# Blocks of one chunk from each sequence in a fused state-space and feed-forward kernel, with its first decays spread by TensorE

## The chip, the cores and the metric

The kernel runs on one core of a Trainium2 chip. The metric is the device time of one execution in microseconds; the span of a profile (first to last instruction) is about 1.8 us shorter than the time of the same execution.

## The reference

Two stages. The first is a scan over sequences (4 sequences, 8 heads, 768 positions, head dimension 32, state 16); the second a mixture of four feed-forward networks on its 3072 rows of 256.

```python
# stage 1, for each chunk; the result does not depend on the chunk length
L = np.exp(cum[:, :, :, None] - cum[:, :, None, :]) * causal   # products of decays a
M = np.einsum('bhin,bhjn->bhij', Cc, Bc) * L
y = np.einsum('bhij,bhjd->bhid', M, xc)                        # from within the chunk
y += np.einsum('bhin,bhnd->bhid', Cc, state) * decay_to_i      # from the chunks before it
state = decay_full * state + np.sum(Bx, axis=2)
# stage 2
p = domain_probs / (domain_probs.sum(-1, keepdims=True) + 1e-09)
for e in range(4):
    out += p[:, e:e + 1] * (np.maximum(x @ w1[e], 0.0) @ w2[e])
```

All is float32. Only the last line of stage 1 ties a chunk to the one before it, and only within a sequence.

## The kernel before

The kernel cuts the sequences into 24 chunks of 128 positions (6 for each sequence) and works in 6 blocks of 4 chunks, 512 rows. While block k goes through stage 2, the chunks of block k+1 go through stage 1 between its products. Stage 2 takes 8 weight steps a block. From the third step on it forms a 2 by 2 block product with seven products instead of eight, for which sums of weights are needed. GpSimd (POOL in the profile) makes these once, in block 0, and stores them for the later blocks. The first two steps of block 0 use eight plain products, because the sums are not there yet.

```python
    def sums_of(op):                       # POOL, 16 times (8 steps, two weight matrices)
        nc.gpsimd.tensor_add(op(S1), op(S3), op(A22))
        nc.gpsimd.tensor_sub(op(S2), op(S1), op(A11))
        nc.gpsimd.tensor_sub(op(S4), op(A12), op(S2))
        nc.gpsimd.tensor_sub(op(S3), op(A11), op(S3))

    def load_decays(c, queue):             # 8 heads x 128 decays, broadcast to 128 partitions: 512 KB
        ab = load.tile([P, NH * P], FP32, tag="ab", name="ab")
        nc.sync.dma_start(out=ab, in_=cut[c].rearrange("h s -> (h s)").partition_broadcast(P))
        if c % chunks_per_seq:             # decays by rows, only where a state comes in
            ...
    def decays(c):
        ...
        nc.vector.tensor_tensor_scan(out=LT, data0=s["ab"], data1=ident..., op0=mult, op1=add)
        ...                                # DVE: products of decays, 2.29 us
        if c % chunks_per_seq:
            nc.vector.tensor_tensor_scan(out=dec, data0=s["ah"], data1=zeros, initial=1.0, ...)
            nc.gpsimd.tensor_mul(cts, s["ctm"], dec...)

    def outputs(c, pool, tag):
        first = c % chunks_per_seq == 0
        if not first:                      # the "state product", 2 records on TensorE
            nc.tensor.matmul(out=y[:, :, 0:P], lhsT=state["M"]..., rhs=s["cts"], ...)
        for t in range(NT):
            for q in range(NQ):            # 16 records
                nc.tensor.matmul(out=y[32 * q:32 * q + 32, t, 0:w], lhsT=xb[...], rhs=MT[...], ...)
        nc.scalar.copy(out=yT[k][...], in_=y[:, :, 0:P])
```

A record is one entry of the profile; each float32 product of TensorE leaves two here.

The opening of the program, where TensorE has nothing to do but wait for the first chunks:

```python
    store_decays(); masks(0)
    turn(2)                # "turn" is a warm-up product whose result nobody reads
    scores(0, homes)
    turn(1)
    ...
    decays(0); masked(0, range(NQ)); masks(1); outputs(0, ...); store_gates()
    scores(1, homes)
    turn(3)
    decays(1); carry(0); masked(1, range(NQ)); masks(2); outputs(1, ...)   # carry: the state
    scores(2, homes)
    plain_first(0, 1)      # the first feed-forward product
```

And the end, where both halves of the last copy read one PSUM tile:

```python
        nc.vector.tensor_copy(rows[0][:, 0], turned[0][:, 0])
        nc.sync.dma_start(out=dst(0)[:, 0], in_=rows[0][:, 0])
        nc.scalar.copy(out=rows[0][:, 1], in_=turned[0][:, 1])
        nc.scalar.dma_start(out=dst(0)[:, 1], in_=rows[0][:, 1])
```

## Time and profile before

| | before |
|---|---|
| time, median of 3 runs | 662.41 us (661.87 to 662.48) |
| span of the profile | 659.3 us |
| TensorE busy | 647.0 us of it (98%) |
| first feed-forward product starts | 19.56 us |
| first half of the plain products over | 37.45 us |
| last products done, first transposition of the result starts | 653.09 us |
| last copy and store issue | 655.84 and 656.24 us |

Four marks of this table return for every run: the **first product**, the **half** (the start of the fourth group of plain first products, where the first 24 second products are over), the sum of the **waits** of TensorE for DVE between 45 and 118 us (block 0; here 0.15 + 0.87 + 0.30 + 0.64 + 0.16 = 2.12 us), and the **end mark**, the first transposition of the result. Since TensorE is busy nearly throughout, a microsecond that moves one mark should move all later ones. The lines of the page and of the opening are in the prediction; its 2.0 for output stores and 4.4 for a 96 KB load are us from issue to landing.

### The profile page before, as it was taken

The page shows a single profiled execution, that of the slowest core. Times are in us where ns is not written, and L with a number is a line of the kernel's source. Part 1 is how long each engine was busy: PE and PEld are TensorE (multiplying, and loading weights), DVE is VectorE, ACT ScalarE, POOL GpSimd, SP SyncE. Part 2 cuts the span into 40 slices and gives each one's busy share as a digit, 9 for nine tenths or more (in the row PEclk, how much of TensorE's full clock was granted, in tenths as well). Part 3 has the DMA queues.
Part 4 walks back from the last instruction along what each step waited for, and adds up shares of the span by engine and source line. Part 5 has one row for each costly group of instructions (what it writes and reads, how often), then busy time and mean ns, then how long its engine had stood idle before and what let it go on. Part 6 is the DMA issues. An engine that isn't in the chain of part 4 may idle for free.

```text
span 659.3 us, 8708 instructions
## 1 busy us (share of the span) xinstructions
PE 647.0 (98%) x3341; PEld 538.3 (82%) x3341; DVE 490.4 (74%) x787; ACT 115.3 (17%) x246; POOL 111.6 (17%) x153
## 2 busy tenths in 40 slices
PE   7999999999999999999999999999999999999997
PEld 2787887888888888888888888888888888888886
DVE  6857898788677688776778867768967776856655
ACT  2101111122112121121122111112211212111110
POOL 2487795030000002000003000001100000200000
PEclk9999999999999999999999999999999999999999
DMA  8975998646736444855372855554573443463100
GB/s 274 344 309 216 301 377 319 218 161 188 264 121 256 160 163 102 309 213 180 127 262 81 263 191 196 204 182 146 163 280 148 153 175 152 114 247 151 56 1 32
DMA packets 67145, 128.62 MB, mean 195 GB/s; under 512 B 24736, under 2 KB 48672, under 8 KB 67104
## 3 DMA queue, kind: packets, MB, share of 16 engines
q1 hardware_dynamic: 64208, 112.92, 50.3%
q0 software_dynamic: 2304, 14.68, 5.5%
q8 instruction: 26, 0.43, 0.2%
q10 hardware_dynamic: 592, 0.48, 0.2%
q14 instruction: 15, 0.12, 0.1%
HBM read 109.99 MB, written 18.07 MB: 194 GB/s over the span
## 4 chain that ended last, share of the span: by engine, by line
PE 87%; DVE 7%; issue 1%; DMA 1%; ACT 0%; DVEq 0%; SPq 0%
PE acc L440 39%; PE X L356 22%; PE Y L356 18%; DVE hT L385 2%; PE acc L421 2%; PE g L273 2%; PE y L301 1%; DVE MT L283 1%; DVE LT L239 1%; PE y L295 1%; DMA wt<-w_d 1%; PE X L404 1%; PE Y L404 1%; DVE z L368 1%; DVE h L378 1%
## 5 line engine op out<-in xcount | busy, mean ns | idle before, releaser
L440 PE MATMUL acc<-hT,wt 128*128 128x256 f32 x736 | 183.2, 382 | 0.0
L368 DVE TENSOR_TENSOR z<-Y,snap 128x512 f32<-128x512 f32 x138 | 95.0, 688 | 112.5 <-ACT snap L363 87.7
L363 ACT COPY snap<-X 128x512 f32<-128x512 f32 x138 | 80.9, 586 | 469.3 <-PE X L356 467.3
L440 PEld LDWEIGHTS acc<-hT,wt 128*128 128x128 f32 x736 | 138.2, 190 | 24.3 <-issue 6.3
L356 PE MATMUL X<-yS,wt 128*128 128x256 f32 x552 | 141.7, 379 | 0.0
L440 PE MATMUL acc<-h,wt 128*128 128x256 f32 x552 | 141.5, 379 | 0.0
L356 PEld LDWEIGHTS X<-yS,wt 128*128 128x128 f32 x552 | 104.9, 190 | 14.3
L440 PEld LDWEIGHTS acc<-h,wt 128*128 128x128 f32 x552 | 104.9, 190 | 14.3
L378 DVE SCALAR_TENSOR_TENSOR h<-z,gate 128x512 f32<-128x512 f32 x138 | 98.1, 711 | 3.2
L356 PE MATMUL Y<-yT,wt 128*128 128x256 f32 x368 | 94.8, 380 | 0.7 <-DVE z L368 0.6
L356 PEld LDWEIGHTS Y<-yT,wt 128*128 128x128 f32 x368 | 68.6, 190 | 12.3 <-DVE z L368 1.5
L385 DVE TENSOR_TENSOR hT<-h,hT 128x512 f32<-128x512 f32 x92 | 70.7, 768 | 3.2
L385 DVE TENSOR_TENSOR hT<-h,h 128x512 f32<-128x512 f32 x92 | 62.7, 717 | 0.7
L246 POOL TENSOR_TENSOR MT<-xb,LT 128x128 f32<-128x128 f32 x20 | 8.3, 415 | 317.1 <-issue 142.4
L239 DVE TENSOR_TENSOR_SCAN LT<-ab,ident 128x1024 f32<-128x1024 f32 x24 | 55.9, 2329 | 0.4
L356 PE MATMUL Y<-yS,wt 128*128 128x256 f32 x184 | 49.4, 391 | 2.0 <-DVE z L368 1.9
L283 DVE TENSOR_TENSOR MT<-g,LT 128x256 f32<-128x256 f32 x96 | 33.9, 415 | 20.9 <-PE g L273 20.8
L356 PE MATMUL X<-yT,wt 128*128 128x256 f32 x184 | 47.3, 380 | 0.9 <-DVE MT L283 0.9
L378 DVE SCALAR_TENSOR_TENSOR h<-X,gate 128x512 f32<-128x512 f32 x50 | 34.5, 691 | 10.4 <-PE X L356 5.7
L356 PEld LDWEIGHTS Y<-yS,wt 128*128 128x128 f32 x184 | 33.2, 189 | 10.9 <-DVE z L368 4.2
L356 PEld LDWEIGHTS X<-yT,wt 128*128 128x128 f32 x184 | 34.9, 190 | 6.0 <-DVE MT L283 1.3
L257 POOL TENSOR_TENSOR cts<-ctm,dec 128x256 f32<-128x256 f32 x20 | 14.7, 737 | 70.3 <-DVE dec L254 69.8
(82 smaller groups left out, 331.8 us busy)
## 6 DMA issues: line engine op xcount, KB each, us to landing
wt<-w_d SPq DMA_DIRECT2D x80, 896.0 KB, 6.3
w_d<-wt POOLq DMA_DIRECT2D x16, 896.0 KB, 6.9
ab<-acut_d SPq DMA_DIRECT2D x22, 512.0 KB, 10.9
wt<-in_w_dram SPq DMA_DIRECT2D x32, 256.0 KB, 5.9
xb<-in_xbc_dram SPq DMA_DIRECT2D x24, 320.0 KB
gate<-p_d SPq DMA_DIRECT2D x24, 256.0 KB, 7.0
out_dram<-ot SPq DMA_DIRECT2D x40, 64.0 KB, 2.0
ah<-ac_d SPq DMA_DIRECT2D x19, 64.0 KB
```

The costliest lines, as they stand in the source:

```text
L239: nc.vector.tensor_tensor_scan(out=LT, data0=s["ab"], data1=ident.rearrange("p h s -> p (h s)"), initial=0.0, op0=ALU.mult, op1=ALU.add)
L257: nc.gpsimd.tensor_mul(cts, s["ctm"], dec.unsqueeze(1).to_broadcast([HN, NT, P]))
L273: nc.tensor.matmul(out=g.rearrange("p t s -> p (t s)"), lhsT=s["xb"][k, OBT:OBT + P], rhs=s["ctm"][k].rearrange("p t s -> p (t s)"), start ...
L283: nc.vector.tensor_mul(s["MT"][:, h, 0:P], s["g"][q], s["LT"][:, h])
L356: nc.tensor.matmul(out=f[bank][:, j], lhsT=wt1[n][:, w, j * P:j * P + P], rhs=rhs, start=(i in (1, 2, 5) and j == 0), stop=(j == JJ - 1), ...
L363: nc.scalar.copy(out=s, in_=first[n]["X"])
L368: nc.vector.tensor_add(z, first[n]["Y"], first[n][i])
L378: nc.vector.scalar_tensor_tensor(out=h, in0=first[n][src], scalar=0.0, in1=g.unsqueeze(1).to_broadcast([P, JJ, HB]), op0=ALU.max, op1=ALU. ...
L385: nc.vector.tensor_sub(h[o], h[x], h[y])
L404: nc.tensor.matmul(out=f[bank][:, j], lhsT=wt1[n][:, w, j * P:j * P + P], rhs=yT[k][:, i, cols], start=(i == 0 and j == 0), stop=(i == 1), ...
L421: nc.tensor.matmul(out=acc[k, u][:, half], lhsT=w2_op(n, w)[:, j], rhs=hid[n][f"{i + 1}{b}"][:, j], start=(begins and i == 0 and j == 0), ...
L440: nc.tensor.matmul(out=acc[k, u][:, half], lhsT=w2_op(n, w)[:, j], rhs=rhs[:, j], start=(begins and j == 0), stop=(n % SPB == SPB - 1 and ...
```

## The change

A block now takes one chunk from each of the four sequences instead of four chunks of one. So block 0 holds only first chunks, which have no state to take in, and the states leave the chain of the opening. The decays of the first two chunks are no longer broadcast by DMA (512 KB each), but loaded small (two loads of 8 KB) and spread over the partitions by TensorE into PSUM. The gates of the first step are spread in the same way. Results of the inner blocks are stored chunk by chunk (160 stores of 16 KB instead of 40 of 64 KB), and the last two copies read separate PSUM banks.

```diff
+    def real(c):                                  # which chunk of the input is chunk c
+        return c % CPB * NBLK + c // CPB
 ...
     def load_tokens(c):
-        nc.sync.dma_start(out=xb, in_=xbc[c])
+        nc.sync.dma_start(out=xb, in_=xbc[real(c)])
     def load_decays(c, queue):
-        ...                                       # 512 KB for every chunk
-        if c % chunks_per_seq:
+        if c >= SPREAD: ...                       # SPREAD = 2
+        if c >= CPB: ...
 ...
+    a_q = const.tile([P, SPREAD, NT, P], FP32, name="a_q")
+    nc.gpsimd.memset(a_q, 0.0)
+    for t, queue in enumerate((nc.sync, nc.scalar)):
+        queue.dma_start(out=a_q...[:, t], in_=a...[0][:, 0:SPREAD])
 ...
+    def spread(c):
+        if c == 0:                                # four row tiles
+            for q, (pool, tag) in enumerate(((ps_f, "X"), (ps_f, "Y"), (ps_s, "acc2"), (ps_s, "acc3"))):
+                nc.tensor.matmul(out=b, lhsT=ones[k], rhs=a_q[k, c]..., tile_position=(32 * q, 0))
+            return
+        b = [ps_f.tile([P, 2, NT * P], FP32, tag=tag, name="a") for tag in ("X", "Y")]
+        for q in range(NQ):                       # four whole products
+            nc.tensor.matmul(out=b[q // 2][:, q % 2], lhsT=qmask[:, q, 0:1].to_broadcast([P, P]),
+                             rhs=a_q[:, c]..., start=(q % 2 == 0), stop=True)
     def decays(c):
+        for i, b in enumerate(s["a"] if c < SPREAD else (s["ab"],)):     # the scan in pieces
+            nc.vector.tensor_tensor_scan(out=LT[:, i * w:i * w + w], data0=b, ...)
 ...
     def outputs(c, pool, tag):
-        first = c % chunks_per_seq == 0
+        k, i = divmod(c, CPB)
+        first = k == 0
 ...
+    turn(1); spread(0); turn(1, 2); masks(0); scores(0, homes); decays(0); spread(1); divide_gates()
+    ...
+    masked(0, range(NQ)); masks(1); scores(1, banks); decays(1)
+    store_gates(); outputs(0, ps_att, "att"); masks(2)
+    ...
+    turn(2)
+    masked(1, range(NQ)); outputs(1, ps_att, "att")
+    scores(2, banks); plain_first(0, 1)
 ...
-                turned[b] = ps_att.tile([P, 2, DM], FP32, tag="att", name="turned")
+                turned[b] = [ps_f.tile([P, DM], FP32, tag=tag, name="turned") for tag in "XY"] if b == 0 else ...
 ...
-            leave(k - 1, 0, BLK, both)
+            turned_out(k - 1)
+        if k > 0 and 1 <= r <= CPB:
+            leave(k - 1, r - 1)
```

## The prediction

> **What bounds the kernel now.** I read the page's busy table first, then the waits of TensorE, then stretches of ten microseconds, and last the timeline of the opening.
>
> ```profile
> PE 647.0 (98%) x3341; PEld 538.3 (82%) x3341; DVE 490.4 (74%) x787; ACT 115.3 (17%) x246; POOL 111.6 (17%) x153
> PE   7999999999999999999999999999999999999997
> ...
> 0.00:10.00 10.00, 6.61 (x14) 2.02 (x14) 5.31 (x21) 2.97 (x6) 2.83 (x14) 1.00 0.79 269
> 10.00:20.00 10.00, 9.17 (x60) 3.96 (x60) 9.56 (x20) 2.34 (x9) 1.52 (x3) 1.00 0.94 293
> 20.00:30.00 10.00, 9.89 (x62) 7.71 (x61) 9.62 (x20) 0.61 (x3) 5.08 (x9) 1.00 1.09 348
> ...
> 300.00:310.00 10.00, 10.00 (x65) 8.22 (x58) 5.96 (x11) 2.22 (x5) 0.00 (x0) 1.00 0.68 228
> ```
> In the stretches the columns are PE, PEld, DVE, ACT and POOL busy. TensorE is the bound from about 20 us on: 10.00 of 10.00 in most stretches. All its idle time is 659.3 - 647.0 = 12.3 us, of which 3.4 + 0.8 lie in the first 20 us and 4.1 after 650 us. But weight loads cover only 2.0 and 4.0 us of the first two stretches, and DVE is full from 10 us on: there TensorE is "busy" with something else. The form of line L550 tells what: twelve warm-up records, 9.6 us, whose result nobody reads.
>
> ```profile
> L550 PE MATMUL w<-ident 128*128 128x512 f32 x12 | 9.6, 893 | 2.4 <-POOL ident L177 2.2
> ...
> 6.77 2.29 DVE L239 TENSOR_TENSOR_SCAN LT<-ab,ident 128x1024 f32<-128x1024 f32 x1
> 9.17 1.42 DVE L283 TENSOR_TENSOR MT<-g,LT 128x256 f32<-128x256 f32 x4
> 12.43 2.29 DVE L239 TENSOR_TENSOR_SCAN LT<-ab,ident 128x1024 f32<-128x1024 f32 x1
> 15.84 1.41 DVE L283 TENSOR_TENSOR MT<-g,LT 128x256 f32<-128x256 f32 x4
> 17.06 0.67 PE L295 MATMUL y<-cts,M 128*128 128x256 f32 x2 [0.58 <-DVE MT L283]
> 17.66 0.70 PE L301 MATMUL y<-MT,xb 128*32 128x144 f32 x16
> 19.56 1.99 PE L404 MATMUL X<-yT,wt 128*128 128x256 f32 x8
> ...
> 32.17 5.45 PE L421 MATMUL acc<-h,wt 128*128 128x256 f32 x24
> 37.45 1.89 PE L404 MATMUL X<-yT,wt 128*128 128x256 f32 x8
> ```
> Columns: start, length, engine, line, operation, operands; in brackets the idle time before it and what ended it. L239 scans the decays of a chunk, L283 masks its scores, L295 applies the state, L301 gives its output, L404 and L421 are the feed-forward products of the first two weight steps. Their first half is over at 37.45 us, my second reference point. The first feed-forward product starts only at 19.56 us. The useful TensorE work before it is 1.24 + 0.88 + 0.29 + 1.11 + 0.67 + 0.70 + 1.34 = 6.2 us, so 13.3 us are lost there. DVE's chain sets this: decays land, clip, scan of chunk 0, masking, clip, scan of chunk 1, state, masking, output. The other losses are small:
>
> ```profile
> PE Y L356 <- DVE z L368: 2.6, 7, 0.6
> PE X L356 <- DVE MT L283: 0.9, 1, 0.9
> ...
> 655.38 0.42 DVE L519 COPY rows<-turned 128x256 f32<-128x256 f32 x1 [0.53 <-PE turned L489]
> 655.84 0.37 ACT L521 COPY rows<-turned 128x256 f32<-128x256 f32 x1 [0.61 <-DVE rows L519]
> ```
> At the end ACT's copy waits for DVE's copy of the same tile before the last store.
>
> [...]6.61 us PE busy in the first stretch, weight loads 2.02, and nearly all of it warm-up. [...]16 records of 144 columns take 0.70 us (one after the other, at 0.216 us per 256 columns, they would be 1.94). The first spread uses such row tiles. [...]a scan takes 2.81 us at 47.97 while a POOL addition beside it takes 2.59 instead of 0.73. [...]The trace has 2.0 for output stores, but 4.4 for the 96 KB load behind the 512 KB broadcast.
>
> **The change, part by part.**
>
> *Decays of chunks 0 and 1 by TensorE.* Two broadcasts of 512 KB and one of 64 KB go out of the DMA queues; two small loads come in. The small loads wait for a POOL memset of 128x512 (from 0.74 us, 128x128 took 0.205; estimate 0.55), so issue at 1.3, landing some 2.3 later: 3.6. Clips of 128x128 at about 0.15 each: 4.4. Four row-tiled products, first one read about 0.9 later: 5.3. The scan in four pieces: 2.29/4 plus about 0.1 fixed each, 2.7: ends 8.0, against 9.06 before.
>
> *DVE from there.* Before: between the end of the first scan and the end of the second masking 17.25 - 9.06 = 8.2 us. Now: reciprocal 0.3, masking 1.42, scan of chunk 1 in two pieces 2.4, masking 1.42 = 5.5. Gone from between: the sums of the gates, the clip of 1024 columns (0.69), the clip and scan of the row decays (0.20 + 0.62), transposition and state (0.18 + 0.29), and their waits. Second masking ends at 13.5 instead of 17.25.
>
> *TensorE up to the first feed-forward product.* Added: two spreads, a gate transposition that is only moved, four gate products, 2 warm-ups in front of output 1 (each 4 x 128 columns, 0.87 or more). I run it on: scores 1 follow the freed banks and are over at 9.6; gate transposition and products to 11.5; output 0 to 12.3; warm-ups to 14.1; output 1, without its state product, to 14.8; scores 2 to 15.9. So the first feed-forward product at 15.9 instead of 19.56: 3.7 us.
>
> *From there to the end of the plain products.* Before, two state products (0.53 each) and a DVE that is full lie in the stretch. Now: product 3.45, output 2 0.65, scores 3 with the copy that frees their bank 1.5, product 3.5, second product 1.7, output 3 0.6, three second products 5.2: 15.9 + 16.6 = 32.5. Before they ended at 37.45. Gain 4.95 us. DVE in the same stretch: clip and scan of chunk 2 to 16.6, masking 18.0, gate 18.7, scan 21.0, gate 21.7, masking 23.1; it is ahead of the banks that TensorE needs (21.5).
>
> *Paid back later.* State products are 20 in both (24 chunks less 4 first ones), but before three of them were in block 0; now chunks 6, 12 and 18 have them instead, 0.53 each = 1.6. Chunk 12's falls into an idle 0.60 us at 254.14 and 0.16 of chunk 6's into that at 107.42, so about 0.9 net. Chunk 6's row-decay scan (0.4 to 0.9) comes on DVE where TensorE already waits 0.64 at 96.89: 0.5.
>
> *The end.* Separate banks for the two halves take ACT's copy out from behind DVE's: 655.84 - 655.38 = 0.45 gained.
>
> *Stores chunk by chunk.* 160 issues instead of 40, the same bytes. The page's issue list has 40 at 64 KB; now 16 KB each. At about 0.35 us of SP time, 8 in each of four steps are 2.8 us of a step of 12.1 to 13, after that step's weight loads; chunk loads have over 20 us of slack (issued 275.98, scanned three steps later). 0.
>
> Sum: 4.95 - 0.9 - 0.5 + 0.45 = 4.0 us; 662.4 - 4.0 = 658.4.
>
> **The rivals.** *The new chain is TensorE's or ACT's.* The gate products, warm-ups and output 0 share two buffers with ACT copies between them. If each hand-over costs 0.3 more, or the clock is low after the early gap, the first product starts at 17.5: gain 3.4 at the plain products, 660 in all. For it speaks that the warm-ups stand ahead of output 1; against it that DVE was 96% busy there. *Queueing in the small loads.* If they land at 5, like the 96 KB load, all is 1.3 later: 659.7. Against: nothing is queued ahead of them now. *The stores.* If 24 more issues per block held up weight loads, each of five blocks would lose a microsecond or more: 663 to 668. Against: TensorE never waits for a weight load in the list of waits. *More than I count.* If starting earlier with 1.3 MB less to move also removes the DVE waits in block 0 (2 to 3 us in all), 656.
>
> **Range and chances.** The opening can be off by 1.5 us either way, the later stalls by 1. So 656.0 to 661.0 around 658.4. A 2% gain is 13.2 us, more than all idle time, so it would need the stall of the opening and much besides; a 2% loss would need the store rival at its worst. 0.01 faster, 0.98 same, 0.01 slower.
>
> **What would show it.** The timeline should have the first scan piece near 5.3, the second masking over near 13.5, the first feed-forward product near 15.9 and the first half of the plain products (L421 x24 before) over near 32.5. State products of chunks 6, 12, 18 should be in the timeline, and the wait near 97 should be somewhat longer. The last two copies should start together. It is wrong if weight loads appear among TensorE's waits, if the first product is later than 17.5, or if blocks 1 to 5 get longer by other than the three state products.

## The result, and the profile after

| | before | after |
|---|---|---|
| median time of the same rounds | 662.28 us (661.87 to 662.48, 4 runs) | 661.17 us (660.69 to 661.72, 4 runs) |
| span | 659.3 us | 658.9 us |
| first product | 19.56 | 17.73 |
| half | 37.45 | 34.57 |
| waits, 45 to 118 us | 2.12 | 3.59 |
| end mark | 653.09 | 652.51 |
| last copy starts | 655.84 | 654.80 |

The ratio is 0.9984 with an interval of 0.9967 to 1.0002. The time is within 2% as predicted, but the gain is 1.1 us and not 4.0, and 661.17 lies just outside the predicted range. A later repeat gave 660.40 (0.9969, 0.9952 to 0.9985), so the gain is 1 to 2 us.

First the timeline of the opening after the change (start, length, engine, line, operation, operands, in brackets the idle time before it). L289 and L296 are the two spreads, L311 the scan, L354 the masking, L266 the gate products, L373 the outputs, L628 the warm-ups, L475 the plain first products.

```profile
4.53 1.24 PE L289 MATMUL a<-a_q,ones 32*128 32x256 f32 x8 [1.40 <-DVE a_q L228]
5.82 2.43 DVE L311 TENSOR_TENSOR_SCAN LT<-a,ident 128x256 f32<-128x256 f32 x4 [0.88 <-PE a L289]
8.12 3.35 PE L296 MATMUL a<-a_q,qmask 128*128 128x256 f32 x8
...
10.29 2.44 DVE L311 TENSOR_TENSOR_SCAN LT<-a,ident 128x512 f32<-128x512 f32 x2 [0.57 <-PE a L296]
...
12.65 1.39 DVE L354 TENSOR_TENSOR MT<-g,LT 128x256 f32<-128x256 f32 x4
12.71 1.16 PE L266 MATMUL gp<-p_sb,ident 96*128 96x128 f32 x8 [0.35 <-ACT p_sb L261]
...
17.73 1.99 PE L475 MATMUL X<-yT,wt 128*128 128x256 f32 x8
...
34.57 1.89 PE L475 MATMUL X<-yT,wt 128*128 128x256 f32 x8
```

DVE did what the prediction said: its first scan piece starts at 5.82 (5.3 predicted), and the second masking is over at 12.65 + 1.39 = 14.04 (13.5; 17.25 before). But the first product starts 3.7 us after that. The chain of waits of the same stretch (start, length, what) shows who holds it:

```profile
8.19 3.28 PE a L296 x8
11.47 0.64 PE g L344 x8
12.11 0.26 PE pp L259
12.39 0.27 ACT p_sb L261
12.71 1.17 PE gp L266 x8
13.90 0.59 ACT gate L270
14.54 1.98 PE t L628 x4
16.53 0.63 PE y L373 x16
17.15 0.64 PE g L344 x8
17.80 1.92 PE X L475 x8
```

From 8.19 us on it is TensorE itself, with two hand-overs to ACT. The largest piece is the second spread: eight records in 3.28 us, 0.41 us each, where a 256-column record takes 0.216 us later on. It runs at about half speed, nearly to its end.

The lead over the kernel before is 1.83 us at the first product and 2.88 at the half, and only 0.58 at the end mark. So 2.30 us are lost between 37 and 652 us, most of it in block 0, as the waits say. Here is the last collision of block 0 in the two timelines, before and then after. The columns are as above. L239 and L311 are the scan of a chunk's decays, L254 and L325 the scan of its row decays, L356 and L427 a feed-forward product, POOL's lines are weight sums and their store.

```profile
107.42 1.13 PE L356 MATMUL Y<-yS,wt 128*128 128x256 f32 x4 [0.16 <-DVE z L368]
107.65 0.57 POOL L161 DMA_DIRECT2D w_d<-wt  x1 [0.30 <-POOL wt L150]
108.01 2.29 DVE L239 TENSOR_TENSOR_SCAN LT<-ab,ident 128x1024 f32<-128x1024 f32 x1
110.21 0.40 DVE L254 TENSOR_TENSOR_SCAN dec<-ah,zeros 128x128 f32<-128x128 f32 x1
111.24 1.13 PE L356 MATMUL Y<-yT,wt 128*128 128x256 f32 x4
```

```profile
105.98 2.81 DVE L311 TENSOR_TENSOR_SCAN LT<-ab,ident 128x1024 f32<-128x1024 f32 x1
106.72 2.59 POOL L161 TENSOR_TENSOR wt<-wt 128x256 f32<-128x256 f32 x1
108.72 0.88 DVE L325 TENSOR_TENSOR_SCAN dec<-ah,zeros 128x128 f32<-128x128 f32 x1
110.23 1.13 PE L427 MATMUL Y<-yT,wt 128*128 128x256 f32 x4 [1.46 <-DVE z L439]
110.41 0.57 POOL L173 DMA_DIRECT2D w_d<-wt  x1 [0.30 <-POOL wt L162]
```

Before, POOL issues the store of its last sums at 107.65, and the scan that follows at 108.01 has its normal 2.29 us; the row scan 0.40. After, the scan comes 2 us earlier, while POOL's chain ends 2.8 us later. They meet: the scan takes 2.81, the addition 2.59 instead of 0.73, the row scan 0.88, and TensorE waits 1.46 us.

At the end, the two copies now start together and the last store is issued about 1.0 us earlier (655.21 against 656.24), of which 0.58 is the earlier end mark:

```profile
654.68 0.39 SPq L586 DMA_DIRECT2D out_dram<-rows  x1
654.70 0.43 DVE L590 COPY rows<-turned 128x256 f32<-128x256 f32 x1 [0.42 <-PE turned L562]
654.80 0.37 ACT L592 COPY rows<-turned 128x256 f32<-128x256 f32 x1
...
655.21 0.38 ACTq L593 DMA_DIRECT2D out_dram<-rows  x1
```

Yet from the end mark to the end of the span it is 658.9 - 652.51 = 6.4 us, and before 659.3 - 653.09 = 6.2.

### The profile page after: what moved, and what is told of

It reads as the page before. It is cut to its first block, busy times and chain, and to the rows that moved or that the text cites. A ratio compares the mean times of both kernels' runs of the same rounds, so it can differ in the third digit from the quotient of the medians.

```text
span 658.9 us, 8898 instructions
## 1 busy us (share of the span) xinstructions
PE 646.9 (98%) x3361; PEld 540.9 (82%) x3361; DVE 493.8 (75%) x790; ACT 115.9 (18%) x247; POOL 117.3 (18%) x161
## 4 chain that ended last, share of the span: by engine, by line
PE 90%; DVE 7%; DMA 1%; issue 1%; ACT 0%; POOL 0%; DVEq 0%; SPq 0%; POOLq 0%
PE acc L511 39%; PE X L427 22%; PE Y L427 18%; PE g L344 2%; PE acc L492 2%; DVE hT L456 2%; PE y L373 2%; DVE LT L311 1%; PE X L475 1%; DVE z L439 1%; PE Y L475 1%; DMA wt<-w_d 1%; PE y L367 1%; DVE MT L354 1%; DVE h L449 1%
## 5 line engine op out<-in xcount | busy, mean ns | idle before, releaser
L427 PE MATMUL X<-yS,wt 128*128 128x256 f32 x552 | 141.7, 379 | 0.0
L427 PEld LDWEIGHTS X<-yS,wt 128*128 128x128 f32 x552 | 104.9, 190 | 14.3
L427 PE MATMUL Y<-yT,wt 128*128 128x256 f32 x368 | 94.9, 380 | 1.8 <-DVE z L439 1.7
L427 PEld LDWEIGHTS Y<-yT,wt 128*128 128x128 f32 x368 | 68.6, 189 | 13.7 <-DVE z L439 3.0
L456 DVE TENSOR_TENSOR hT<-h,h 128x512 f32<-128x512 f32 x92 | 63.2, 723 | 0.7
L311 DVE TENSOR_TENSOR_SCAN LT<-ab,ident 128x1024 f32<-128x1024 f32 x22 | 52.3, 2379 | 0.1
L427 PE MATMUL Y<-yS,wt 128*128 128x256 f32 x184 | 49.3, 390 | 2.3 <-DVE z L439 2.3
L354 DVE TENSOR_TENSOR MT<-g,LT 128x256 f32<-128x256 f32 x96 | 33.9, 415 | 20.9 <-PE g L344 20.9
L427 PE MATMUL X<-yT,wt 128*128 128x256 f32 x184 | 47.3, 380 | 0.5 <-DVE MT L354 0.5
L427 PEld LDWEIGHTS Y<-yS,wt 128*128 128x128 f32 x184 | 33.3, 189 | 10.9 <-DVE z L439 4.3
L427 PEld LDWEIGHTS X<-yT,wt 128*128 128x128 f32 x184 | 34.9, 190 | 5.6 <-DVE MT L354 0.9
```

Of the source, the lines that this page charges most:

```text
L311: nc.vector.tensor_tensor_scan(out=LT[:, i * w:i * w + w], data0=b, data1=ident.rearrange("p h s -> p (h s)")[:, :w], initial=0.0, op0=ALU ...
L354: nc.vector.tensor_mul(s["MT"][:, h, 0:P], s["g"][q], s["LT"][:, h])
L427: nc.tensor.matmul(out=f[bank][:, j], lhsT=wt1[n][:, w, j * P:j * P + P], rhs=rhs, start=(i in (1, 2, 5) and j == 0), stop=(j == JJ - 1), ...
L456: nc.vector.tensor_sub(h[o], h[x], h[y])
```

## The experiments

Two questions. Why did the first product start at 17.73 and not at 15.9? And where between 37 and 652 us did 2.3 us go?

For the second, the first theory (T1 here, "Theory 1" in the expectations) was: TensorE and DVE now run ahead of POOL's chain of weight sums, more of DVE's scans and gate operations meet POOL's additions, both take longer there (in the kernel before, at 47.97 us, a scan took 2.81 us instead of 2.29 and the addition beside it 2.59 instead of 0.73), and TensorE waits. The rivals, each named in the expectation of the run that tests it, were the added state work of chunk 6, the other new work of block 1's chunks, a late start of POOL, and the stores.

The table has one trace for each run and the times of its rounds. All are compared with the kernel before, timed on the same chip in the same rounds (medians 662.3 to 662.5). The edits are against the changed kernel unless it is said otherwise.

| run | first product | half | waits | end mark | time | ratio (interval) |
|---|---|---|---|---|---|---|
| before | 19.56 | 37.45 | 2.12 | 653.09 | 662.28 | |
| before, again (b1) | 19.98 | 38.03 | 1.74 | 653.31 | 661.33 | one look |
| after | 17.73 | 34.57 | 3.59 | 652.51 | 661.17 | 0.9984 (0.9967 to 1.0002) |
| after, again (a1) | 17.74 | 34.58 | 3.78 | 652.72 | 660.40 | 0.9969 (0.9952 to 0.9985) |
| e1 no warm-up | 16.39 | 33.24 | 3.59 | 651.30 | 659.77 | 0.9971 (0.9957 to 0.9985) |
| e2 spread of chunk 0 only | 18.98 | 35.82 | 2.62 | 653.01 | 661.57 | 0.9997 (0.9984 to 1.0010) |
| e15 gap filled | 18.15 | 34.99 | 3.06 | 652.68 | 660.92 | 0.9981 (0.9948 to 1.0014) |
| e17 tokens early | 15.90 | 32.74 | 2.77 | 651.27 | 660.33 | 0.9974 (0.9955 to 0.9993) |
| e3 zero sums, after | 18.32 | 35.16 | 0.66 | 649.13 | 657.14 | 0.9924 (0.9912 to 0.9936) |
| e4 zero sums, before | 21.63 | 39.33 | 0.66 | 652.38 | 659.71 | 0.9965 (0.9951 to 0.9980) |
| e5 chunk 6 stateless | 17.73 | 34.58 | 3.55 | 651.86 | 660.89 | 0.9977 (0.9955 to 1.0000) |
| e16 light block 1 | 17.76 | 34.60 | 3.74 | 651.51 | 659.28 | 0.9957 (0.9941 to 0.9973) |
| e12 weights before gate | 18.44 | 35.28 | 3.42 | 652.62 | 660.76 | 0.9976 (0.9958 to 0.9993) |
| e6 early sums | 17.17 | 34.01 | 3.00 | 651.37 | 660.16 | 0.9964 (0.9945 to 0.9983) |
| e9 early sums, no warm-up | 16.48 | 33.98 | 3.03 | 651.39 | 659.89 | 0.9973 (0.9949 to 0.9998) |
| e10 three edits | 15.76 | 35.54 | 3.00 | 652.90 | 660.81 | 0.9986 (0.9955 to 1.0016) |
| e18 delayed start | 21.10 | 37.94 | 2.79 | 655.30 | 662.52 | 0.9996 (0.9981 to 1.0012) |
| e8 stores at once | 17.90 | 35.74 | 3.08 | 653.42 | 661.22 | 0.9989 (0.9963 to 1.0015) |
| e14 tail in one bank | 18.35 | 35.19 | 4.23 | 654.22 | 661.62 | 0.9983 (0.9966 to 1.0000) |
| e19 all together | 16.60 | 33.44 | 3.07 | 650.87 | 658.93 | 0.9949 (0.9935 to 0.9963) |

One caution is in the table itself. Runs e3, e8 and e14 leave the opening as it was, and their half is 35.16 to 35.74 against 34.57 and 34.58 of the two runs of the changed kernel. So one trace can be off by about 1 us in the opening. The kernel before has it too: 37.45 and 38.03, and 39.33 in e4. In e3 and e14 it goes with the moment at which TensorE's clock comes up (12.33 and 12.25 us instead of 10.90), shown under e15; in e8 TensorE waits 1.25 us for the tokens of chunk 3.

### The opening

**e1: without the two warm-up products before output 1.**

```diff
-    turn(2)
     masked(1, range(NQ))
```

> The two warm-up products before output 1 are gone; nothing else differs. Both theories: the first feed-forward product starts near 15.8 us instead of 17.73, if the clock holds. Theory 1 (an earlier start is taken back in weight steps 2 to 7, where DVE and POOL hold each other off and TensorE waits for DVE): under half of that, 0.9 us or less, is left at the end, and the waits on line z between 55 and 115 us add up to more than the 3.6 us of the changed kernel. Theory 2 (the shortfall is fixed extra work, chunk 6's state product and row decays, and an earlier start carries through): 1.9 us or so off the end, near 659.3. Rival for the opening: without the warm-ups the clock is low and the first product gains less than 1 us.

The first product starts 1.34 us earlier, at 16.39, with the full clock from 11.17; what stops it there is ACT, and ahead of that TensorE itself (the chain of waits goes from the second spread by the gate products and output 0 to ACT's copy and masks; DVE is not in it). The two TensorE lines from 15 us on:

```profile
15.75 0.71 PE L344 MATMUL g<-ctm,xb 32*128 32x256 f32 x8 [0.38 <-ACT ctm L335]
16.39 1.78 PE L475 MATMUL X<-yT,wt 128*128 128x256 f32 x7
```

The end mark is 1.21 us earlier and the waits are unchanged at 3.59. So a microsecond gained in the opening is passed on to the end nearly whole; it is not halved on the way, as T1 in its first form expected. Running 1.3 us further ahead did not lengthen the waits.

**e2: only chunk 0 spread by TensorE, chunk 1's decays broadcast by DMA again.**

```diff
-    SPREAD, DIRECT = 2, 3
+    SPREAD, DIRECT = 1, 3
...
     nc.scalar.dma_start(out=pr, in_=probs)
+    load_decays(1, nc.sync)
     load_tokens(1)
...
     decays(0)
-    spread(1)
     divide_gates()
```

> Only chunk 0's decays are spread by TensorE; chunk 1's come by broadcast load as in the kernel before. If the four K=128 spread products (3.35 us in the trace) are what delays the opening, the first feed-forward product starts near 16.2 instead of 17.73, although DVE gets a clip of 0.76 us more. If the opening is bound by DVE or by loads, it starts at 17.7 or later. At the end: theory 1 at most half of the gain, theory 2 all of it.

A miss. The 512 KB went ahead of chunk 1's tokens, whose masks then waited 2.60 us, and TensorE stood idle where the spread had been. What came after ran slower:

```profile
11.79 2.08 PE L267 MATMUL gp<-p_sb,ident 96*128 96x128 f32 x8 [0.35 <-ACT p_sb L262]
...
14.92 2.86 PE L629 MATMUL t<-ones 128*128 128x512 f32 x4
```

The same gate products took 1.16 us after the change, the same warm-ups 1.98. So the spread could not be saved in this way: it costs 3.3 us, but where TensorE idled in its place, what followed was slower (one trace). The traces show two speeds of TensorE, 0.42 and 0.216 us for a record of 256 columns. When the clock comes up is looked at under e15; in e2's trace it does so only at 16.71 us, within the second of the lines above.

**e15: one more warm-up product in the idle time before the first spread.**

```diff
     turn(1)
+    turn(1, 2)
     spread(0)
```

> One more half-sized warm-up in the gap of 1.4 us ahead of the first spread. If the second spread (3.35 us, 0.42 us a record where warm records of that form take 0.216) is slow because TensorE's clock has not come up, it takes 1.7 to 2.5 us now and the first feed-forward product starts up to 1.5 us sooner than 17.73. If it is slow by its form, it stays at 3.3.

A miss. The idle time before the first spread fell from 1.40 to 0.57 us, and the second spread took 3.75 us instead of 3.35:

```profile
8.14 3.75 PE L296 MATMUL a<-a_q,qmask 128*128 128x256 f32 x8
```

But this does not show that the gap is without effect, because the moment at which the clock comes up also differs between runs. The packed traces list the changes of the granted clock. The first entry of each is the full clock, and the query program prints 1.00 for the time before it, so the clock column reads 1.00 from 8 to 12 us and hides the low clock. The length of the second spread follows that first entry:

| run | full clock from (us) | second spread (us) |
|---|---|---|
| e17 | 9.08 | 2.54 |
| e18 | 9.29 | 2.64 |
| e8 | 9.96 | 2.90 |
| after, a1 | 10.90, 10.94 | 3.35, 3.38 |
| e1 | 11.17 | 3.53 |
| e15 | 11.73 | 3.75 |
| e14 | 12.25 | 3.78 |

In b1 the clock was full from 5.59, halved from 9.00 and full again from 12.41, two steps of 3.41 us. The other changes fit whole multiples of such a step, called ticks below: the next change after 10.90 comes 648.53 us later, which is 190 times 3.413, and in e15 it is 189 times. Where these ticks fall in the kernel differs from run to run: e8 and e14 have the same opening, and their clock came up at 9.96 and 12.25. So e15 had a late tick, 11.73, and what filling the gap does stays open. The runs with the changed kernel's opening show that the slow spread is on the path: the first product starts at 17.73 to 17.76 where the clock came up at 10.90 to 11.04 (after, a1, e5, e16), and at 18.35 and 18.32 where it did at 12.25 and 12.33 (e14, e3). The exception is e8, 17.90, whose gate transposition waits 0.58 us for POOL.

**e17: chunk 3's tokens loaded with the first loads (a fourth buffer), and no warm-ups.**

```diff
-        xb = load.tile([P, W], FP32, tag="xb", name="xb")
+        xb = load.tile([P, W], FP32, tag="xb", name="xb", bufs=4)
...
     load_tokens(2)
+    load_tokens(3)
...
-    load_tokens(3)
...
-    turn(2)
```

> Correct result. Four token buffers, chunk 3's tokens loaded at the start, and no warm-ups ahead of output 1. In the changed kernel the masks of chunk 3 start at 20.6 us after 2.95 us of ACT idle for that load. The first feed-forward product should start near 16.4, the second plain first-half (X) near 21.0 instead of 23.28, the first half of the plain products be over near 32; time 658.8 to 659.8.

First product 15.90, half 32.74: the predicted 15.9 and 32.5 almost exactly, with the second spread still in place. Part of this is luck: the clock came up at 9.08, so the spread took 2.54 us and not e1's 3.53. But the end mark is 651.27, no earlier than e1's 651.30, though e1 was half a microsecond later at the half and waited 0.82 us more in block 0. The waits do not list what was lost instead: after a wait of 1.69 us the granted clock fell to half for 3.41 us, and eight records took 0.427 us instead of 0.216, about 1.7 us in all. The line (`prof e17_tokens3_early --windows 56.87:60.28`) has the columns of the stretches in the prediction; the clock is the third number from the end:

```profile
56.87:60.28 3.41, 3.41 (x10) 2.70 (x8) 3.38 (x4) 1.18 (x3) 3.01 (x5) 0.50 0.19 80
```

This trace also shows most plainly how long a DVE operation can take beside POOL:

```profile
53.40 0.42 POOL L320 TENSOR_TENSOR MT<-xb,LT 128x128 f32<-128x128 f32 x1
53.59 2.14 DVE L450 SCALAR_TENSOR_TENSOR h<-z,gate 128x512 f32<-128x512 f32 x1
53.78 0.72 POOL L329 TENSOR_TENSOR cts<-ctm,dec 128x256 f32<-128x256 f32 x1
54.46 0.71 POOL L159 TENSOR_TENSOR wt<-wt 128x256 f32<-128x256 f32 x1
...
56.12 1.38 PE L428 MATMUL X<-yT,wt 128*128 128x256 f32 x4 [1.69 <-DVE MT L355]
```

A gate operation, which takes 0.69 us alone, lasts 2.14 us across three POOL operations; the masking behind it is late, and TensorE waits 1.69 us instead of 0.51.

### Where the lead went

**e3 and e4: zeros in place of POOL's weight sums, in the changed kernel and in the one before.** Their outputs are wrong, which doesn't matter for the times. Memory writes of the same size stay, but POOL no longer reads the weights (the expectation calls their memory SBUF). Each of these writes takes 0.30 to 0.34 us where an addition takes 0.73, so POOL is also busy for less time.

```diff
     def sums_of(op):
-        nc.gpsimd.tensor_add(op(S1), op(S3), op(A22))
-        nc.gpsimd.tensor_sub(op(S2), op(S1), op(A11))
-        nc.gpsimd.tensor_sub(op(S4), op(A12), op(S2))
-        nc.gpsimd.tensor_sub(op(S3), op(A11), op(S3))
+        for w in (S1, S2, S4, S3):
+            nc.gpsimd.memset(op(w), 0.0)
```

> Wrong result on purpose: POOL writes zeros where it added and subtracted weights, so it reads no SBUF there and is done sooner. Theory 1: the waits on line z in weight steps 2 to 7 (3.6 us) go away nearly wholly, scans are back at 2.29 us from 2.8, and the time falls by 3 to 3.5 us, to about 657.8. Theory 2: the waits shrink by under 1.5 us, as DVE's own load stays.

> The same in the kernel before, for the difference of the two changes: theory 1: it gains only its 2.1 us of waits (about 660.2), so that with zeros the change is worth 2 to 2.6 us instead of 1.1. Theory 2: it gains as much as the changed kernel does, and the change stays worth about 1.1 us.

All the waits of block 0 but two go away in both kernels, 0.15 + 0.51 = 0.66 us being left. The last scan of block 0 in e3 has its plain durations again, and the product behind it does not wait:

```profile
102.42 2.28 DVE L309 TENSOR_TENSOR_SCAN LT<-ab,ident 128x1024 f32<-128x1024 f32 x1
...
104.62 0.40 DVE L323 TENSOR_TENSOR_SCAN dec<-ah,zeros 128x128 f32<-128x128 f32 x1
...
106.95 1.03 PE L425 MATMUL Y<-yT,wt 128*128 128x256 f32 x4
```

In e3 five gate operations ran beside POOL's memory writes and took their usual 0.69 us; no scan met one. With the sums in place, in the changed kernel, a scan grew from 2.28 us to 2.81 (at 105.98) and 3.32 (at 46.22), a row scan from 0.40 to 0.88 and an addition of POOL from 0.73 to 2.59; in e17 a gate operation grew from 0.69 to 2.14. In the time of the whole kernel the sums cost about 2.8 us in the kernel before (662.48 to 659.71, e4) and 3.3 to 4.0 in the changed one (660.40 or 661.17 to 657.14, e3).

Without the sums the change is worth 659.71 - 657.14 = 2.57 us by the medians; with them 1.1 in the first comparison and about 1.9 in the repeat. The times alone do not separate these (e4's six spread over 2.3 us); the marks do better. From the half to the end mark the changed kernel is 2.30 us longer than the one before with the sums (617.94 against 615.64) and 0.92 without them (613.97 against 613.05). So 1.38 of the 2.30 us go with POOL's sums and their meeting with DVE. The 0.92 that remain are about the net of the three added state products (worked out below). This is the clearest pair, though each number is one trace: the same stretch takes 618.14 us in a1, 617.68 in e8, 619.03 in e14 and 615.28 in b1.

The sums cost more than the listed waits (615.64 - 613.05 = 2.59 us in the kernel before, of which 2.12 - 0.66 = 1.46 are waits). Set record against record, the traces with and without sums drift apart only at TensorE's stalls in block 0: before at 60.0, 80.1, 92.5, 96.9, 107.4 and 111.2 us, 2.59 us in all, and after at 63.2, 67.0, 93.9, 105.1 and 110.2 us, 3.98 in all. So a stall costs up to 0.37 us more than its listed idle time, three of them (92.5 and 111.2 before, 67.0 after) are too short for the list, and nothing is lost elsewhere.

**e5: chunk 6 treated as a first chunk** (wrong): no row decays, no state product. It stands where the prediction expected half a microsecond of new wait.

```diff
-        if c >= CPB:                    # in load_decays, decays and carry
+        if c >= CPB and c != 6:
...
-        first = k == 0
+        first = k == 0 or c == 6
```

> Wrong result on purpose: chunk 6 is treated as the first of its sequence, as in the kernel before (no state product of 0.53 us, no row-decay scan, no scaling on POOL, no load of its row decays). If chunk 6's work [...]is what made the waits grow, the waits of TensorE between 45 and 115 us fall from 3.59 to about 2.1 us, as in the kernel before, and the time falls by 1.5 to 2 us, to near 659.3. If the growth is an accident of how POOL's sums fall against the scans, only the product and the scan themselves go: under 1 us.

A miss for that rival: the waits are 3.55 instead of 3.59. The end mark is 0.65 us earlier with an equal half, which is chunk 6's own work.

**e16: block 1 lightened further**, chunk 5 makes no state, chunks 6 and 9 take none in (wrong).

```diff
-        if c >= CPB:
+        if c >= CPB and c != 6:         # load_decays and decays
...
-        if c < NCH - CPB:
+        if c < NCH - CPB and c != 5:
...
-        first = k == 0
+        first = k == 0 or c in (6, 9)
```

> Wrong result on purpose: block 1 has the work that it had in the kernel before: chunk 5 makes no state (no POOL product, no carry of about 1 us on DVE), chunk 6 uses none, and so that it can run, chunk 9 uses none either (one product of 0.53 us less in a later block). If the work that the new order puts into block 1 is the cause, the waits between 43 and 115 us fall to about 2.1 us and the time to 659.0 or so. If they stay at 3 or more, the cause is how the sums fall, not the work.

A miss as well: 3.74. The growth of the waits does not come from the amount of new work on DVE or TensorE in block 0's steps.

**e12: the weights of step 2 loaded before the second gates**, so that POOL's chain starts earlier.

```diff
-    load_gate(0, 1)
     load_w1(2)
     load_w2(2)
+    load_gate(0, 1)
     turn(2)
```

> Correct result. POOL's first weight sum started at 26.47 us in the kernel before and at 26.43 in the changed one, though TensorE was 2.9 us ahead: the load of that weight stands behind a gate load that waits for the gates' store. Here the weights of step 2 are issued ahead of that gate. Theory 3 (POOL's chain of sums is pinned by loads, so a TensorE that runs ahead meets more of it): the first sum starts near 24, the sums end 2 us sooner, and the waits of TensorE between 45 and 115 us fall from 3.59 towards the 2.1 of the kernel before; time 659.8 or so. If the waits do not depend on POOL's start, no change within 0.4 us.

POOL's first sum starts at 25.28 instead of 26.43, but its chain still ends near 110.5, and the waits are 3.42. When POOL begins is not what decides. That its later additions wait for later weights and are stretched by the collisions is likely, but not tested.

**e6: twelve of POOL's additions moved into the opening**, where POOL is idle.

```diff
     turn(2)
+    early_w1(0)          # the first three sums of w1(0); the fourth stays where it was
+    early_w1(1)
     masked(1, range(NQ))
...
     decays(2)
+    early_w2(0)
     masked(2, range(NQ))
...
     load_chunk(5)
+    early_w2(1)
     gated(0, "11", "X")
```

> Correct result. The first three of four sums of the weights of steps 0 and 1 (12 POOL additions, 9 us) are moved from 38 to 62 us to the time between 13 and 26 us in which POOL waits. Theory 1 (DVE and POOL hold each other off in weight steps 2 to 7): POOL is done about 9 us sooner, the waits between 45 and 115 us fall from 3.59 to 2.2 or less, and the time falls by 1 to 2 us. If DVE's own load is the reason, the waits stay above 3 us. The risk: scans of the opening at 2.8 us instead of 2.29.

The waits are 3.00 instead of 3.59, the end mark is 1.14 us earlier, and the result stays correct. But 0.56 of the 1.14 are there at the half already (the clock came up at 9.81), and e8 and e15, which moved no sum, wait 3.08 and 3.06. So one trace does not show what the early sums give; four with early sums (e6, e9, e10, e19) agree on 3.00 to 3.07 where the other traces of the new order with all their sums lie between 2.62 and 4.23. It is half of a cure at best: twelve of 64 additions left block 0, and the rest still meet DVE.

**e9: e6 without the two warm-ups.**

```diff
-    turn(2)
+    early_w1(0)
+    early_w1(1)
     masked(1, range(NQ))
```

(with e6's other edits)

> Correct result. Early sums, and without the two warm-up products. If the two gains are independent they add: 1.4 us of the first plus what the early sums give, 1 to 2 us: 658.0 to 659.0, ahead of both kernels. If POOL's sums in the opening slow the scans, which set the pace once the warm-ups are gone, it is no better than 659.8.

No better than e6. The first product is earlier (16.48), but the early sums stand in POOL's queue ahead of its small part of chunk 2, so output 2 waits 0.59 us for POOL and the half is at 33.98.

**e10: no warm-ups, weights before gate, and early sums in other places.**

```diff
-    load_gate(0, 1)
     load_w1(2)
     load_w2(2)
-    turn(2)
+    load_gate(0, 1)
+    early_w1(0)
...
     decays(2)
+    early_w1(1)
...
     decays(3)
+    early_w2(0)
+    early_w2(1)
```

> Correct result. No warm-ups ahead of output 1, weights of step 2 ahead of the gate, early sums placed so that no output waits for POOL (in the last combination output 2 waited 0.6 us for POOL and the start's gain was lost). First feed-forward product near 16.4, first half of the plain products over near 33, waits between 45 and 115 us at 2.5 or less: 657.8 to 659.0, faster than both kernels.

A miss. The first product is at 15.76, the earliest of all, and the half at 35.54. TensorE then waits 1.49 us for the masks of chunk 3, that is for its tokens, and the products after the wait run at the low clock (2.83 and 2.78 us for eight records instead of 1.99 and 1.89; the trace's clock is half from 23.58 to 26.99). A start that the next chunk's loads cannot follow is not a gain.

**e18: the opposite, five warm-ups instead of two**, so that the plain products end where they did before.

```diff
-    turn(2)
+    turn(5)
```

> Three more warm-ups ahead of output 1, so that the first half of the plain products is over near 37.3 us, as in the kernel before, instead of 34.57. If the growth of the waits is the price of running ahead of POOL's sums, the waits between 45 and 118 us fall from 3.6 to about 2 us, and the end is only some 1.2 us later than the changed kernel's for a start 2.7 us later. If the waits belong to the new order itself, they stay at 3.6 and the end is 2.7 us later.

This was to separate being early from the new order. The half is at 37.94, as before the change (37.45 and 38.03), and the waits are 2.79: between before's 1.74 to 2.12 and after's 3.59 to 3.78. Neither form of the theory is met: with an equal start the waits should have been about 2.0 if running ahead were all of it, and about 3.6 if it were nothing. So with an equal start 0.7 to 1.0 us of extra wait stay with the new order. That the other 0.8 to 1.0 go with the earlier start is not shown: e8, e14 and e15 run the same block 0 with the half at 35.74, 35.19 and 34.99 and wait 3.08, 4.23 and 3.06, so half a microsecond moves the waits as much as e18's three. Further ahead still, e1 and e17 wait 3.59 and 2.77. What repeats is the exact meeting: four traces with the half at 34.57 to 34.60 (after, a1, e5, e16) wait 3.55 to 3.78. What in the order keeps the waits longer is open. e5 and e16 exclude its added work, which leaves the positions at which DVE's scans and POOL's additions happen to meet. That is an argument, not a measurement.

### The other terms

**e8: all 32 stores of a block at once instead of chunk by chunk.**

```diff
-        if k > 0 and 1 <= r <= CPB:
-            leave(k - 1, r - 1)
+        if k > 0 and r == 1:
+            for c in range(CPB):
+                leave(k - 1, c)
```

> The stores of an inner block all go out in one step, 32 issues in a row, instead of 8 in each of four steps. Nothing on the way of TensorE waits for them in the trace, so within 0.4 us of the changed kernel's 661.2 by all theories; if it is more than 1 us slower, the spreading of the stores was needed.

The time is the same (0.9989 against 0.9984), and from the half to the end mark it takes 617.7 us against 617.9. How the stores are grouped costs nothing in this kernel, though the transfers differ: the 160 stores of 16 KB had a median of 6.0 us to landing where they went out step by step with the weight loads, and 1.5 us when issued together; the loads of the stored weights then took 10.4 us instead of 5.8.

**e14: the last two copies from one tile again.**

```diff
-                turned[b] = [ps_f.tile([P, DM], ...) for tag in "XY"] if b == 0 else ps_att.tile(...)
+                turned[b] = ps_att.tile([P, 2, DM], FP32, tag="att", name="turned")
```

> The last two halves are turned into one tile again, as in the kernel before, so ACT's copy waits for DVE's. If the end is set by the 0.5 MB of the three last stores moving at 345 GB/s from the first of them on, the time is the same within 0.2 us; by my prediction it would be 0.45 us longer.

The copies stand one behind the other again:

```profile
656.52 0.42 DVE L589 COPY rows<-turned 128x256 f32<-128x256 f32 x1 [0.53 <-PE turned L561]
...
656.98 0.37 ACT L591 COPY rows<-turned 128x256 f32<-128x256 f32 x1 [0.61 <-DVE rows L589]
```

Yet from the end mark to the end of the span it is 660.5 - 654.22 = 6.3 us, the 6.4 of the changed kernel. The last stores move 0.5 MB, and the first half of it is issued ahead of these copies in both forms. The traces of the two kernels show 342 to 352 GB/s in half-microsecond slices of that stretch, so 0.5 MB take some 1.5 us (an estimate from that rate), and issuing one store 0.45 us sooner gained nothing here. The packets run from 656.16 to 657.83 us before and from 655.59 to 657.25 after, so the last one ends 4.74 us behind the end mark in both.

**b1 and a1: both kernels once more.**

> The kernel before again, for a second trace. If its waits for DVE between 45 and 118 us are again near 2.1 us, the growth in the changed kernel is real; if they come to 3 or more, the first trace was a lucky one and the difference is scatter.

> The changed kernel again, with more rounds: 661.2 within 0.5 us, ratio 0.998 to 0.999; waits between 43 and 115 us of 3.0 to 4.2, as in its near relatives.

Before has waits of 0.15 + 0.51 + 0.29 + 0.63 + 0.16 = 1.74, after 3.78. Every trace of the new order with all its sums waits longer (2.62 to 4.23), so the difference is real and not a chance of one trace; its size is not fixed.

**e19: a version to use.** No warm-ups, chunk 3's tokens early (e17), and nine additions of POOL early, in places where they stand in front of nothing that the opening needs.

```diff
-        xb = load.tile([P, W], FP32, tag="xb", name="xb")
+        xb = load.tile([P, W], FP32, tag="xb", name="xb", bufs=4)
...
     load_tokens(2)
+    load_tokens(3)
...
-    turn(2)
+    early_w1(0)
     masked(1, range(NQ))
...
     decays(3)
+    early_w1(1)
+    early_w2(0)
     gated(0, "21", "Y")
```

> Correct result. No warm-ups ahead of output 1, chunk 3's tokens early, and the first sums of three weights (9 POOL additions) in POOL's idle time of the opening, placed behind POOL's part of chunks 1 and 3. First half of the plain products over near 32.8, waits at 3 or less: 658.3 to 659.8, ahead of both kernels. If running ahead is paid back one for one, it is no better than 660.4.

The first product starts at 16.60, with the clock up only at 11.42. The result is correct and the time 658.93 us, 0.9949 (0.9935 to 0.9963) of the kernel before: 3.4 us by the medians, against 1.1 to 1.9 for the change as it was made. Its six runs, 658.73 to 659.64, lie below all runs of both kernels but one of the changed kernel (659.63 in the repeat). It is faster than the kernel before; against the changed kernel its interval is clear of the first comparison and overlaps the repeat's.

## Why the prediction was right or wrong

The class (within 2%) and the sign were right; of the 4.0 us about 1 to 2 came. In the trace the terms are these:

| term of the sum | predicted | measured |
|---|---|---|
| first product earlier | 3.7 | 1.83 |
| more, up to the half | 1.25 | 1.05 |
| state products of chunks 6, 12, 18, net | -0.9 | -0.9 (e3, e4) |
| waits in block 0 | -0.5 | -1.4 (1.47 listed, 1.38 by e3, e4) |
| end | +0.45 | -0.2 |
| sum, in the span | 4.0 | 0.4 |

**The DVE chain was right.** Second masking over at 14.04 (13.5 predicted), with the small loads landing 2.4 us after their issue at 1.29. The 0.15 us for a clip, the 0.9 to the first read and the 0.1 fixed for a piece of the scan were estimates; the trace after has 0.28 for a clip, 1.29 from the first spread's start to the scan, and 2.43 for the four pieces together, against 2.29 for one scan. e17 reached the predicted 15.9 and 32.5, but by luck: without the warm-ups (1.8 us of the sum) and with an early clock, which together offset the spread.

**The step that failed first: "scores 1 follow the freed banks and are over at 9.6".** They were over at 12.1. Between the two lies the second spread, which the sum gave no time of its own: eight records, mostly at half speed, 3.3 us. At the full clock they would take about 1.7 (an estimate, 8 times 0.216), so about half of the missed time is the spread itself and half the low clock. From there on the sum was right: gate products over 2.4 us late, output 0 2.2, output 1 2.4, scores 2 1.9. It is one mis-sized term, a cost counted as nothing, not a wrong list. The rival "the new chain is TensorE's or ACT's", with 17.5 us and a time of 660, is what happened (17.73 and 661.17 or 660.40). The reason it was given, that warm-ups stand ahead of output 1, was true as well: e1 takes them away and gains 1.34 us. So was its condition of a low clock (0.41 us a record instead of 0.216, the full clock from 10.90 us on); that the gap before it was the cause is not shown (e15). The argument against it, DVE at 96% in that stretch, did not hold, because the change had just emptied DVE's part: an engine that is full before says nothing on who will be the bound after.

**The step that failed second: chunk 6's row scan as the cost in block 0, 0.5 us.** The direction was right, the size a third and the cause another. Listed waits rose by 1.47 us (by 1.85 against the repeat of before). e5 and e16 show that the added work is not the cause, e3 with e4 that the meeting of POOL's sums with DVE is. The prediction quoted such a meeting from the trace, 2.81 us at 47.97, and did not use it: it did not ask what an earlier TensorE would meet. How much of the growth comes from being early, and how much from where scans and additions happen to meet in the new order, stays open; 0.7 to 1.0 us stay with an equal start (e18).

**The state products were sized well.** Compared chunk by chunk, at the starts of their output products, the lead falls by 0.49 us at chunk 6 (4.17 to 3.68 between e4 and e3), by 0.48 at chunk 12 and by 0.49 at chunk 18 (between the two kernels); 0.53 was predicted for each. Chunk 12's wait at 254 us became smaller by 0.43 (0.60 to 0.17 us), as predicted, since its state product fills it.

**The end: wrong.** The prediction read the wait of ACT's copy as time on the path of the end. Behind it stand the last stores, whose packets run for 1.67 us before (656.16 to 657.83, 314 GB/s) and 1.66 after (655.59 to 657.25, 315 GB/s); e14 shows no gain from separate banks (6.3 us from the end mark to the end of the span, against 6.4).

**The stores: right**, by e8 (an issue took 0.43 us in the median, 0.35 predicted). No wait for weight loads came up, and none of the later blocks got longer except by state products: chunk by chunk the lead is 1.01 to 1.02 from chunk 7 to 11, 0.96 from 13 to 17, 0.47 to 0.58 from 18 on.

**One reading was loose.** Of the 6.61 us of TensorE in the first ten about 5.4 are warm-up, and 1.24 the scores of chunk 0; "nearly all" is too much, but nothing hangs on it.

## What to carry to other kernels

Before counting what a removed chain gives, write down the whole chain of the engine that inherits the path, at the clock it will have there: here 3.3 us of mostly half-speed TensorE records (0.41 us instead of 0.216), counted as nothing, halved the lead at the first product. An engine that gets ahead can meet others at other moments, so list which pairs slow each other (here a scan on DVE with an addition on POOL, 2.81 us instead of 2.29 and 2.59 instead of 0.73) and look at what runs where the earlier one will arrive. To find such a loss, compare a few fixed marks along two traces, then take away the suspected partner in both kernels rather than in one. And read when the clock came up in each trace before comparing two openings.
